# An attention and dense-layer kernel: interleaved q and k, four more pairs on DMA transposes and GpSimd pooling, attention ranked first

## Chip, cores, metric

The kernel runs on one core of one Trainium2 chip. The metric is device time in microseconds (us) of one execution. Before the change the median of three runs was 345.75 us (345.23 to 347.05).

## The reference, cut

Batch 8, 8 heads, 576 tokens, head size 64. Two attentions are added, and two dense layers follow.

```python
def _attn_ref(q, k, v):                       # each (8, 8, 576, 64)
    q_d = q.reshape(B, H, Sd, 4, D).mean(axis=3)      # pooled by 4: 144 tokens
    k_d, v_d = ...                                    # the same
    out_up = np.repeat(sm_attn(q_d, k_d, v_d), 4, axis=2)
    mask = np.abs(pos[:, None] - pos[None, :]) < 4    # a narrow band
    scores = np.where(mask, scale * q @ k.T, -1e9)
    ...                                               # softmax
    return out_up + attn @ v

def reference(**kwargs):
    x = attn_out.transpose(0, 2, 1, 3).reshape(4608, 512)
    h = x @ w_in                              # 512 x 2048
    return (h - np.tanh(h)) @ w_out           # 2048 x 512
```

## The kernel before

Two heads of one batch make a pair; there are 32 pairs. Each is loaded, reordered and cast (`qr`), transposed so that the head dimension lies on partitions, copied to `qk`, pooled by four in two additions (`half`, `qkd`), scored on TensorE, exponentiated on ScalarE (`E`), masked on VectorE (from pair 4 on; the first four add a bias on TensorE instead), multiplied with V, normalised (`ln`), transposed back and joined into `xT`, the input of the dense layers. From pair 16 on, DMA does the transposes, GpSimd pools V, and the join adds two SBUF operands. The parts that the argument touches:

```python
full = bass.AP(tensor=qk[s].tensor, ...,              # q, then k, 585 elements on
               ap=[qk[s].ap[0], [KOFF, 2], [1, 576]])
if p >= T_DMA:
    P.dma("SP", 1740, lambda: nc.sync.dma_start_transpose(out=qT[s], in_=qr[s]...), ...)
    for i in range(2):                                # one copy for q, one for k
        op("ACT", 600, lambda i=i: A.copy(out=full[:, i]..., in_=qT[s]...[:, i]), ...)
# ... else: nine TensorE transposes into PSUM and one copy from there
def add1(eng):                                        # first sum: half is (2, G, 2)
    eng.tensor_tensor(out=half, in0=four[:, :, :, 0:2], in1=four[:, :, :, 2:4], op=ALU.add)
def add2(eng):                                        # second sum: stores 288 elements in a row
    eng.tensor_tensor(out=qkd[s][:, 0:2 * G].rearrange("p (i g) -> p i g", i=2),
                      in0=half[:, :, :, 0], in1=half[:, :, :, 1], op=ALU.add)
# ...
if p >= NP:                                           # two mask multiplies a pair: 480+480, then 96+96
    op("DVE", 850, lambda: V.tensor_tensor(out=e1, in0=e1, in1=mask..., op=ALU.mult), ...)
# ... value matmuls, normalisation, transpose back
P.choice([("DVE", 850, lambda: join(V)), ("POOL", 1450, lambda: join(GP))], ...)
# ...
M2_FIRST, T_DMA, X_DMA, NEW = 16, 16, 16, 16
```

Nothing is scheduled at run time. `op` and `choice` record operations with a planned duration (the number) and a rank (`pri`); a list scheduler simulates the engines with those durations, picks the engine where there is a choice, and so fixes every engine's order.

The softmax here doesn't subtract the row's maximum and nothing guards it: scores larger than these inputs give would overflow.

## Time and profile before

| of the kernel before | value |
|---|---|
| median (range) of 3 runs | 345.75 us (345.23 to 347.05) |
| span of the profiled run | 345.9 us |
| value matmuls of pairs 4, 11, 15, 31 start at | 40.7, 92.7, 121.4, 240.4 us |
| dense matmuls in the order after the last value matmul | 468 of 1152 |
| second pooling sum on GpSimd | 711 ns, 29 of 32 |

The last value matmuls divide the run: until then attention and dense layers share TensorE; afterwards dense matmuls alone run at 0.216 us each. The span is the start of the last value matmuls, plus 0.216 us for each dense matmul left, plus some 5 us: here 240.4 + 101.1 + 4.4.

Two groups of the profile before that the prediction does not show, which matter later (columns: line, engine, operation, output<-inputs, shapes, count; busy us and mean ns of one; idle us just before and what ended it):

```profile
L497 POOL TENSOR_TENSOR qkd<-half 128x288 bf16<-128x288 f32 x29 | 20.6, 711 | 1.6 <-DVE half L492 0.7
...
L581 PE MATMUL ps_ox<-vw,E 128*128 128x65 bf16 x300 | 19.2, 194 | 4.6 <-DVE E L570 2.6 <-DVE E L556 1.9
```

The first is the second pooling sum. The second is TensorE's value matmuls, which sat idle 4.6 us in all for masks (L556, L570).

### The profile page before, as it was taken

To read this page: it belongs to the slowest core of one execution; us is meant where nothing else is said; L and a number is where in the kernel's file an instruction comes from. 1 tells how busy PE (TensorE), PEld (TensorE's weight loads), DVE (VectorE), ACT (ScalarE), POOL (GpSimd) and SP (SyncE) were. 2 spreads that over 40 slices of the span, in tenths; PEclk is the share of its full clock that TensorE was granted. 3 is DMA by queue.
4 is the path that set the end of the run, shared out by engine and by line. 5 is a ranking of instruction groups with operands and counts; after the bars stand their busy time and mean duration, and the time that the engine had idled before them with its cause. 6 is when DMAs were issued, how large, how long until landed. Compare 5 with 4: busy or idle time off the path is not lost.

```text
span 345.9 us, 6596 instructions
## 1 busy us (share of the span) xinstructions
PE 324.6 (94%) x2479; PEld 164.0 (47%) x2520; DVE 215.1 (62%) x341; ACT 217.4 (63%) x350; POOL 161.9 (47%) x191
## 2 busy tenths in 40 slices
PE   8888998899999999987989889999999999999995
PEld 4553555455555554443444444445444444444442
DVE  4786774258978577888789889876533443344300
ACT  2966864578888769978577878885443444344411
POOL 7675368364698729889666878641000000000000
PEclk9999999899999999999899999999999999999999
DMA  7999999999779926999999999532201100110021
GB/s 241 271 222 226 235 260 240 274 299 235 205 178 244 253 84 136 213 249 213 267 208 259 236 256 185 154 83 60 58 32 48 43 32 30 51 40 32 30 85 68
DMA packets 99213, 56.52 MB, mean 163 GB/s; under 512 B 77678, under 2 KB 86382, under 8 KB 99182
## 3 DMA queue, kind: packets, MB, share of 16 engines
q1 hardware_dynamic: 94670, 51.32, 60.2%
q0 software_dynamic: 4224, 4.19, 7.5%
q10 hardware_dynamic: 288, 0.59, 0.5%
q8 instruction: 19, 0.31, 0.4%
q14 instruction: 12, 0.10, 0.1%
HBM read 42.46 MB, written 9.44 MB: 150 GB/s over the span
## 4 chain that ended last, share of the span: by engine, by line
PE 66%; DVE 15%; DMA 9%; ACT 4%; issue 3%; POOL 2%; SPq 1%; POOLq 0%; ACTq 0%; DVEq 0%
PE ps_hy L690 27%; PE ps_hy L663 27%; DMA qkn<-in_k_dram 5%; DVE E L556 4%; DMA w_out_sb<-in_moe_w_out_dram 3%; DVE xT L626 2%; PE ps_ox L581 2%; DVE gT L674 2%; DVE ln L602 2%; PE ps_ts L511 2%; PE ps_ts L477 2%; PE ps_ox L588 2%; DVE xT L632 2%; ACT E L552 1%; DVE E L570 1%
## 5 line engine op out<-in xcount | busy, mean ns | idle before, releaser
L663 PE MATMUL ps_hy<-xT,w_in_sb 128*128 128x512 bf16 x555 | 142.4, 382 | 5.2 <-DVE xT L643 1.9
L690 PE MATMUL ps_hy<-w_out_sb,gT 128*128 128x512 bf16 x557 | 141.0, 382 | 3.4 <-DMA w_out_sb<-in_moe_w_out_dram 2.1
L674 DVE TENSOR_TENSOR gT<-ps_hy,u 128x512 bf16<-128x512 f32 x144 | 96.6, 685 | 72.4 <-ACT u L671 71.6
L671 ACT ACTIVATE u<-ps_hy 128x512 f32<-128x512 f32 x144 | 84.4, 600 | 70.8 <-PE ps_hy L663 69.7
L690 PEld LDWEIGHTS <-gT 128*128 128x128 bf16 x576 | 54.5, 98 | 64.5 <-issue 3.0
L663 PEld LDWEIGHTS <-w_in_sb 128*128 128x128 bf16 x576 | 53.6, 98 | 65.0 <-issue 6.3
L492 POOL TENSOR_TENSOR half<-qk 128x576 f32<-128x576 bf16 x29 | 33.7, 1161 | 28.8 <-ACT qk L468 13.7
L447 POOL CAST qr<-qkn 128x1152 bf16<-128x1152 f32 x28 | 33.5, 1198 | 14.7 <-PE ps_ts L477 9.6
L468 ACT COPY qk<-qT 128x576 bf16<-128x576 bf16 x32 | 38.1, 1213 | 0.0
L552 ACT ACTIVATE E<-ps_ts 128x960 bf16<-128x960 f32 x30 | 29.2, 973 | 11.6 <-PE ps_ts L511 11.3
L556 DVE TENSOR_TENSOR E<-E,mask 128x960 bf16<-128x960 bf16 x28 | 27.3, 974 | 13.3 <-ACT E L552 13.0
L602 DVE TENSOR_TENSOR ln<-ps_ox,r 128x896 bf16<-128x896 f32 x30 | 32.7, 1090 | 0.9
L701 ACT COPY y<-ps_hy 128x512 f32<-128x512 f32 x36 | 21.1, 586 | 18.3 <-PE ps_hy L690 14.1
L381 POOL CAST vw<-vst 128x640 bf16<-128x640 f32 x32 | 25.6, 799 | 8.7 <-DMA vst<-in_v_dram 7.1
L481 ACT COPY qk<-ps_ts 128x1152 bf16<-128x1152 bf16 x14 | 15.7, 1124 | 13.9 <-PE ps_ts L477 12.1
L581 PE MATMUL ps_ox<-vw,E 128*128 128x65 bf16 x300 | 19.2, 194 | 4.6 <-DVE E L570 2.6
L581 PEld LDWEIGHTS <-E 128*128 128x128 bf16 x320 | 16.1, 98 | 12.0 <-DVE E L556 4.0
L497 POOL TENSOR_TENSOR qkd<-half 128x288 bf16<-128x288 f32 x29 | 20.6, 711 | 1.6 <-DVE half L492 0.7
L402 POOL TENSOR_TENSOR v<-v 72x512 f32<-72x512 f32 x16 | 20.6, 1287 | 1.4 <-DMA v<-in_v_dram 0.5
L406 POOL TENSOR_TENSOR vp<-v 72x256 bf16<-72x256 f32 x16 | 12.3, 772 | 13.4 <-PE ps_ox L588 13.3
L511 PEld LDWEIGHTS <-qk 64*128 64x128 bf16 x320 | 9.6, 95 | 17.5 <-issue 16.7
L643 DVE TENSOR_TENSOR xT<-ps_ox,od 128x576 bf16<-128x576 bf16 x14 | 10.5, 752 | 8.0 <-ACT od L641 8.0
(90 smaller groups left out, 260.0 us busy)
## 6 DMA issues: line engine op xcount, KB each, us to landing
vst<-in_v_dram SPq DMA_DIRECT2D x62, 160.0 KB, 4.9
qkn<-in_q_dram SPq DMA_DIRECT2D x32, 288.0 KB, 4.7
out_dram<-y SPq DMA_DIRECT2D x36, 256.0 KB, 2.0
qkn<-in_k_dram SPq DMA_DIRECT2D x30, 288.0 KB, 4.6
v<-in_v_dram SPq DMA_DIRECT2D x16, 288.0 KB
w_in_sb<-in_moe_w_in_dram POOLq DMA_DIRECT2D x4, 512.0 KB, 11.1
w_out_sb<-in_moe_w_out_dram POOLq DMA_DIRECT2D x4, 512.0 KB, 10.4
qkn<-in_k_dram ACTq DMA_DIRECT2D x2, 288.0 KB, 3.4
```

Of the source, the lines that this page charges most:

```text
L381: P.choice([(eng, ns, lambda fn=fn: fn(out=vw[w][:, 2 * jj:2 * jj + 2, :, 0:64], in_=vst[s])) for eng, ns, fn in CAST_V[p >= NEARLY]], rea ...
L447: op("POOL", 1300, lambda: GP.tensor_copy(out=qr[s].rearrange("p a (h d) -> p h a d", h=2), in_=qkn[sn].rearrange("p h (a d) -> p h a d", ...
L468: op("ACT", 600, lambda i=i: A.copy(out=full[:, i].rearrange("p (g a) -> p g a", a=A9), in_=qT[s].rearrange("p a (g i) -> p i g a", i=2)[: ...
L492: eng.tensor_tensor(out=half, in0=four[:, :, :, 0:2], in1=four[:, :, :, 2:4], op=ALU.add)
L552: op("ACT", 870, lambda: A.activation(out=e1, in_=ps[:, :, 0:480], func=AF.Exp, scale=SCALE), reads=ts, writes=[("E", e, 0)], pri=pri)
L556: op("DVE", 850, lambda: V.tensor_tensor(out=e1, in0=e1, in1=mask[:, 0:480].unsqueeze(1).to_broadcast([128, 2, 480]), op=ALU.mult), reads= ...
L581: T.matmul(po[:, hh, 65 * t:65 * t + 65], E[e][:, c:c + 128], vw[w][:, 2 * jj + hh, t, :], start=True, stop=True)
L602: op("DVE", 1010, lambda: V.tensor_tensor(out=ln[s].rearrange("p n (h d) -> p h n d", d=D), in0=blocks[:, :, :, 0:64], in1=r[s].unsqueeze( ...
L663: T.matmul(ps_hy[slot], w_in_sb[:, dc, fc * 128:(fc + 1) * 128], xT[dc][:, kb * 512:kb * 512 + 512], start=(dc == 0), stop=(dc == N_DC - 1))
L671: op("ACT", 490, lambda: A.activation(out=u[us], in_=ps_hy[slot], func=AF.Tanh), reads=[("hy", slot)], writes=[("u", us)], pri=-1)
L674: op("DVE", 620, lambda: V.tensor_tensor(out=gT[g][:, fc, :], in0=ps_hy[slot], in1=u[us], op=ALU.subtract), reads=[("hy", slot), ("u", us) ...
L690: T.matmul(ps_hy[slot], gT[g][:, fc, ts * 128:ts * 128 + 128], w_out_sb[:, fc, :], start=(fc == 0), stop=(fc == N_FF - 1))
```

## The change

Four things at once. q and k are interleaved element by element, so that one copy fills both. Pairs 12 to 15 join the later ones in using DMA transposes, merged scores and GpSimd pooling of V. The dense layers' operations on ScalarE, VectorE and the DMA queue lose their rank before attention's (`DPRI`). And the planned durations are brought nearer to the trace. Core of the diff (line numbers shift by 2 or so; guards, keys and more planned durations are cut):

```diff
-    qk = fixed("qk", [128, 1192], BF16, 2)
+    qk = fixed("qk", [128, LEAD + 576 + 28, 2], BF16, 2)
-    half = fixed("half", [128, 2, G, 2], FP32)
+    half = fixed("half", [128, G, 2, 2], FP32)
...
-            for i in range(2):
-                op("ACT", 600, lambda i=i: A.copy(
-                    out=full[:, i].rearrange("p (g a) -> p g a", a=A9),
-                    in_=qT[s].rearrange("p a (g i) -> p i g a", i=2)[:, i]),
-                   reads=[("qT", s)], writes=[("qk", s, i)], pri=pri)
+            op("ACT", 1250, lambda: A.copy(
+                out=full.rearrange("p (g a) i -> p g a i", a=A9),
+                in_=qT[s].rearrange("p a (g i) -> p g a i", i=2)),
+               reads=[("qT", s)], writes=[("qk", s)], pri=pri)
...
-            eng.tensor_tensor(out=half, in0=four[:, :, :, 0:2],
-                              in1=four[:, :, :, 2:4], op=ALU.add)
+            eng.tensor_tensor(out=half, in0=four[:, :, 0:2, :],
+                              in1=four[:, :, 2:4, :], op=ALU.add)
...
-                eng.tensor_tensor(out=qkd[s][:, 0:2 * G].rearrange("p (i g) -> p i g", i=2),
-                                  in0=half[:, :, :, 0],
-                                  in1=half[:, :, :, 1], op=ALU.add)
+                eng.tensor_tensor(out=qkd[s][:, 0:2 * G].rearrange("p (i g) -> p g i", i=2),
+                                  in0=half[:, :, 0, :],
+                                  in1=half[:, :, 1, :], op=ALU.add)
...
-            T.matmul(sc[:, c:c + NQ[t]], qk[s][rows, k0:k0 + 128],
-                     qk[s][rows, QW * t:QW * t + NQ[t]], ...)
+            T.matmul(sc[:, c:c + NQ[t]], qk[s][rows, k0:k0 + 128, 1],
+                     qk[s][rows, q0:q0 + NQ[t], 0], ...)
...
-            P.choice([("DVE", 850, lambda: join(V)), ("POOL", 1450, lambda: join(GP))],
+            P.choice([("DVE", 1900, lambda: join(V)), ("POOL", 1400, lambda: join(GP))],
...
-           reads=[("hy", slot)], writes=[("u", us)], pri=-1)
+           reads=[("hy", slot)], writes=[("u", us)], pri=DPRI)
...
-    M2_FIRST, T_DMA, X_DMA, NEW = 16, 16, 16, 16
+    M2_FIRST, T_DMA, X_DMA, NEW, LATE = 12, 12, 12, 12, 0
+    DPRI = 5000
```

The second sum: its input now has q and k side by side, its output still has all of q before all of k. With `p g i` as the order, it stores q of group 0, then k of group 0, then q of group 1, and so on.

More of the change, by code (lines that the diff above doesn't have):

```diff
@@ L208 @@
     NQ = [120, 120, 120, 120, 96]
-    KOFF = 585
+    LEAD = 4
     N_FF = Dff // 128
@@ L442, in attention @@
         cold = 1.5 if p < NP else 1.0
+        late = LATE if p >= 2 * NP else 0
         yield
@@ L458, in attention @@
                      pri=pri - 12)
-        full = bass.AP(tensor=qk[s].tensor, offset=qk[s].offset,
-                       ap=[qk[s].ap[0], [KOFF, 2], [1, 576]])
+        full = qk[s][:, LEAD:LEAD + 576]
         if p >= T_DMA:
@@ L478, in attention @@
             P.fresh.add(len(P.ops))
-            op("PE", 520 * cold, tr, reads=[("qr", s, 0), ("qr", s, 1), "ident"],
+            op("PE", 520 * cold, tr, slack=late, reads=[("qr", s, 0), ("qr", s, 1), "ident"],
                writes=ts, pri=pri)
             op("ACT", 1240, lambda: A.copy(
-                out=full.rearrange("p i (g a) -> p i g a", a=A9),
-                in_=b16.rearrange("p (a g i) -> p i g a", a=A9, i=2)),
-               reads=ts,
-               writes=[("qk", s, 0), ("qk", s, 1)], pri=pri)
-        four = full.rearrange("p i (g a) -> p i g a", a=4)
+                out=full.rearrange("p (g a) i -> p g a i", a=A9),
+                in_=b16.rearrange("p (a g i) -> p g a i", a=A9, i=2)),
+               reads=ts, writes=[("qk", s)], pri=pri)
+        four = full.rearrange("p (g a) i -> p g a i", a=4)
         adders = ADDERS[p >= NEARLY]
         def add1(eng):
-            eng.tensor_tensor(out=half, in0=four[:, :, :, 0:2],
-                              in1=four[:, :, :, 2:4], op=ALU.add)
+            eng.tensor_tensor(out=half, in0=four[:, :, 0:2, :],
+                              in1=four[:, :, 2:4, :], op=ALU.add)
         def add2(eng):
             with nc.allow_low_precision("pooled q and k"):
-                eng.tensor_tensor(out=qkd[s][:, 0:2 * G].rearrange("p (i g) -> p i g", i=2),
-                                  in0=half[:, :, :, 0],
-                                  in1=half[:, :, :, 1], op=ALU.add)
+                eng.tensor_tensor(out=qkd[s][:, 0:2 * G].rearrange("p (i g) -> p g i", i=2),
+                                  in0=half[:, :, 0, :],
+                                  in1=half[:, :, 1, :], op=ALU.add)
         P.choice([(name, n1, lambda eng=eng: add1(eng)) for name, n1, _, eng in adders],
-                 reads=[("qk", s, 0), ("qk", s, 1)], writes=["half"], pri=pri)
+                 reads=[("qk", s)], writes=["half"], pri=pri)
         P.choice([(name, n2, lambda eng=eng: add2(eng)) for name, _, n2, eng in adders],
@@ L509, in score @@
             rows = slice(64 * hh, 64 * hh + 64)
-            k0 = KOFF + QW * t - 4
-            T.matmul(sc[:, c:c + NQ[t]], qk[s][rows, k0:k0 + 128],
-                     qk[s][rows, QW * t:QW * t + NQ[t]], start=p >= NP, stop=p >= NP or t >= 3)
+            k0, q0 = LEAD + QW * t - 4, LEAD + QW * t
+            T.matmul(sc[:, c:c + NQ[t]], qk[s][rows, k0:k0 + 128, 1],
+                     qk[s][rows, q0:q0 + NQ[t], 0], start=p >= NP, stop=p >= NP or t >= 3)
         def biased(lo, hi):
@@ L539, in s12 @@
             s2(po.rearrange("p n c -> p (n c)"), 72)
-        qks = [("qk", s, i) for i in range(2)]
+        qks = [("qk", s)]
         yield
@@ L544, in attention @@
         if new:
-            op("PE", 620, s12, reads=qks + [("qkd", s)], writes=ts + ox, pri=pri)
+            op("PE", 620, s12, slack=late, reads=qks + [("qkd", s)], writes=ts + ox, pri=pri)
         else:
-            op("PE", 420 * cold + 600 * (p < NP), s1,
+            op("PE", 420 * cold + 600 * (p < NP), s1, slack=late,
                reads=qks + ["bias"] * (p < NP), writes=ts, pri=pri)
@@ L551, in attention @@
         e3 = E[e][:, 1152:1728].rearrange("p (h c) -> p h c", h=2)
-        op("ACT", 870, lambda: A.activation(
+        op("ACT", 960, lambda: A.activation(
             out=e1, in_=ps[:, :, 0:480], func=AF.Exp, scale=SCALE),
@@ L555, in attention @@
         if p >= NP:
-            op("DVE", 850, lambda: V.tensor_tensor(
+            op("DVE", 950, lambda: V.tensor_tensor(
                 out=e1, in0=e1,
@@ L561, in attention @@
         if not new:
-            op("PE", 380 * cold + 150 * (p < NP), s2, reads=qks + [("qkd", s)], writes=ts, pri=pri)
-        op("ACT", 240, lambda: A.activation(
+            op("PE", 380 * cold + 150 * (p < NP), s2, slack=late, reads=qks + [("qkd", s)], writes=ts, pri=pri)
+        op("ACT", 310, lambda: A.activation(
             out=e2v, in_=ps2[:, :, 0:96], func=AF.Exp, scale=SCALE),
            reads=ts2, writes=[("E", e, 1)], pri=pri)
-        op("ACT", 560, lambda: A.activation(
+        op("ACT", 650, lambda: A.activation(
             out=e3, in_=ps2[:, :, 96:384], func=AF.Exp, scale=SCALE / 16.0),
@@ L569, in attention @@
         if p >= NP:
-            op("DVE", 300, lambda: V.tensor_tensor(
+            op("DVE", 450, lambda: V.tensor_tensor(
                 out=e2v, in0=e2v,
@@ L594, in attention @@
         P.fresh.add(len(P.ops))
-        op("PE", 570 * cold, outs,
+        op("PE", 570 * cold, outs, slack=late,
            reads=[("E", e, 0), ("E", e, 1), ("E", e, 2), ("vw", w, jj),
@@ L601, in attention @@
            reads=ox, writes=[("r", s)], pri=pri)
-        op("DVE", 1010, lambda: V.tensor_tensor(
+        op("DVE", 1060, lambda: V.tensor_tensor(
             out=ln[s].rearrange("p n (h d) -> p h n d", d=D),
@@ L636, in join @@
                     op=ALU.add)
-            P.choice([("DVE", 850, lambda: join(V)), ("POOL", 1450, lambda: join(GP))],
+            P.choice([("DVE", 1900, lambda: join(V)), ("POOL", 1400, lambda: join(GP))],
                      reads=[("lT", s)], writes=[("x", b, j)], pri=pri)
             return
-        op("PE", 370 * cold, back, reads=[("ln", s)], writes=ox, pri=pri)
+        op("PE", 370 * cold, back, slack=late, reads=[("ln", s)], writes=ox, pri=pri)
         op("ACT", 190, lambda: A.copy(out=od[s], in_=px[1][:, 0:144]),
@@ L670, in mm1 @@
                writes=[("hy", slot)], pri=5000)
-        op("ACT", 490, lambda: A.activation(
+        op("ACT", 590, lambda: A.activation(
             out=u[us], in_=ps_hy[slot], func=AF.Tanh),
-           reads=[("hy", slot)], writes=[("u", us)], pri=-1)
-        op("DVE", 620, lambda: V.tensor_tensor(
+           reads=[("hy", slot)], writes=[("u", us)], pri=DPRI)
+        op("DVE", 670, lambda: V.tensor_tensor(
             out=gT[g][:, fc, :], in0=ps_hy[slot], in1=u[us], op=ALU.subtract),
-           reads=[("hy", slot), ("u", us)], writes=[("gT", g, fc)], pri=-1)
+           reads=[("hy", slot), ("u", us)], writes=[("gT", g, fc)], pri=DPRI)
     ycur = {}
@@ L700, in mm2 @@
             yn[0] += 1
-            op("ACT", 490, lambda: A.copy(out=y[ys], in_=ps_hy[slot]),
-               reads=[("hy", slot)], writes=[("y", ys)], pri=-1)
+            op("ACT", 590, lambda: A.copy(out=y[ys], in_=ps_hy[slot]),
+               reads=[("hy", slot)], writes=[("y", ys)], pri=DPRI)
             r0 = kb * 512 + ts * 128
             P.dma("SP", 530, lambda: nc.sync.dma_start(
-                out=out[r0:r0 + 128, :], in_=y[ys]), 700, 344, src=[("y", ys)], pri=-1)
+                out=out[r0:r0 + 128, :], in_=y[ys]), 700, 344, src=[("y", ys)], pri=DPRI)
     def dense(kb):
@@ L745, in guards @@
         def guards(i=i):
-            V.memset(qk[i][:, 576:585], 0.0)
-            V.memset(qk[i][:, 1161:1192], 0.0)
+            V.memset(qk[i][:, 0:LEAD], 0.0)
+            V.memset(qk[i][:, LEAD + 576:LEAD + 604], 0.0)
         op("DVE", 200, guards, pri=-98,
-           writes=[("qk", i, a) for a in range(2)])
+           writes=[("qk", i)])
     for i in range(NVW):
```

## The prediction

> **What bounds the kernel now.** I read the page's busy shares and slices first, then a table of stretches, then the groups by line, then the chain of waits.
>
> From the page: busy shares, then the span in 40 slices of 8.65 us.
>
> ```profile
> PE 324.6 (94%) x2479; PEld 164.0 (47%) x2520; DVE 215.1 (62%) x341; ACT 217.4 (63%) x350; POOL 161.9 (47%) x191
> ...
> PE   8888998899999999987989889999999999999995
> ...
> POOL 7675368364698729889666878641000000000000
> PEclk9999999899999999999899999999999999999999
> DMA  7999999999779926999999999532201100110021
> ```
>
> TensorE is busy all along, at full clock but for two slices; GpSimd works until slice 28 (240 us); the DMA engines are full until about slice 25, with a dip at 14 and 15 (121 to 138 us). So there are two phases: attention with the dense layers mixed in, then dense layers alone. The table of stretches, cut where the value matmuls (L581) of pairs 11, 15 and 31 start in the timeline (92.7, 121.4, 240.4 us), gives busy time and number of instructions of each engine, then clock, DMA share and GB/s:
>
> ```profile
> 27.50:92.70 65.20, 62.10 (x566) 34.14 (x576) 41.27 (x66) 44.94 (x77) 35.26 (x40) 0.97 1.04 251
> 92.70:121.40 28.70, 28.38 (x266) 15.51 (x268) 20.80 (x33) 23.56 (x39) 24.62 (x26) 1.00 0.91 220
> 121.40:240.40 119.00, 111.15 (x917) 54.78 (x932) 97.10 (x139) 93.13 (x142) 81.48 (x86) 0.99 0.86 189
> 240.40:342.10 101.70, 101.17 (x477) 46.26 (x485) 36.53 (x56) 38.52 (x67) 0.56 (x2) 1.00 0.12 44
> ```
>
> The last row is the bare rate: the built program's order has 468 dense matmuls of 512 columns after the last value matmul, 101.1 us at 0.216 us each (chain of waits: x8 in 1.73 us). The kernel is **TensorE work plus TensorE's holes**: all 1152 dense matmuls are 248.8 us, attention's own TensorE work some 60 (16 pairs x 2.74 + 16 x 1.05, both worked out below), and the rest of 346 us is holes, start and a 3.8 us tail. The third row shows where a hole can be saved: pairs 16 to 31 take 119 us, in which the order has 412 dense matmuls (89.0 us) and 16 x 1.05 us of attention (16.8; in the timeline merged scores take 0.48, values 0.57), so 13.2 us, 0.83 us per pair, are holes. The second row, pairs 12 to 15 with TensorE transposes, has hardly any.
>
> Groups by line (count | busy us, mean ns of one | idle before it and its releaser):
>
> ```profile
> L468 ACT COPY qk<-qT 128x576 bf16<-128x576 bf16 x32 | 38.1, 1213 | 0.0
> L481 ACT COPY qk<-ps_ts 128x1152 bf16<-128x1152 bf16 x14 | 15.7, 1124 | 13.9 <-PE ps_ts L477 12.1 <-POOL qr L447 1.8
> L402 POOL TENSOR_TENSOR v<-v 72x512 f32<-72x512 f32 x16 | 20.6, 1287 | 1.4 <-DMA v<-in_v_dram 0.5
> L556 DVE TENSOR_TENSOR E<-E,mask 128x960 bf16<-128x960 bf16 x28 | 27.3, 974 | 13.3 <-ACT E L552 13.0
> L626 DVE TENSOR_TENSOR xT<-lT 128x480 bf16<-128x480 bf16 x11 | 12.8, 1167 | 1.6 <-DMA lT<-ln 1.6
> L626 POOL TENSOR_TENSOR xT<-lT 128x480 bf16<-128x480 bf16 x5 | 5.1, 1012 | 7.8 <-DMA lT<-ln 7.8
> ```
>
> The first two rows are the oddity that the interleaving is after: two copies of 576 elements from SBUF cost 2.43 us, one of 1152 from PSUM 1.12. The chain in this phase runs mostly through VectorE:
>
> ```profile
> 161.93 2.13 DVE E L556
> ...
> 177.05 2.62 DVE xT L626
> ```
>
> The same mask multiply takes 0.64 us at its shortest and 2.76 at its longest, the join 0.65 to 2.62 (view of one line). So in pairs 16 to 31 VectorE (97.1 of 119 us), slowed by something, makes TensorE's holes.
>
> [...] 216 start to start in the dense runs, 56 inside the nine transposes. [...] In L468 each two-byte element read lies 256 bytes from the next; 2.1 ns per element against 0.98 for L481[...]. [...]
>
> **The change, part by part.**
> 1. *TensorE transposes removed for pairs 12 to 15.* In the timeline near 84 to 93 us: nine transposes into PSUM 0.51 us (92.24 to 92.75), seven back 0.75 (89.56 to 90.31), V pooling 0.66 per two pairs, so 0.33, and split scores 0.58 against merged 0.48. Together 1.69 us a pair, 6.8 us in all. It lies on TensorE, the bound.
> 2. *What these pairs take on.* GpSimd: V pooling, 1.29 + 0.77 us a pair. VectorE or GpSimd: a join (VectorE 1.17 + 0.74, GpSimd 1.01 + 0.35) for the PSUM join (0.75). DMA: 0.82 MB more a pair, by the tiles' sizes: V again 0.295, transpose in 0.295, out 0.229. They also take on the holes of the later pairs: 4 x 0.5 to 0.8 us, 2 to 3 us. Net of parts 1 and 2: some 4 us gained.
> 3. *Interleaving.* One ScalarE copy (I take 1.2 us) for two (2.43): 16 x 1.2 = 19 us of ScalarE, beside other work. On the path it shortens the wait GpSimd's half sums have for it (11.1 us in five waits between 140 and 240 us), so the scores come earlier. GpSimd's sums keep their sizes; the second now writes strided, and I leave it at 0.71.
> 4. *Order.* Joins in the order: VectorE 11 to 10, GpSimd 5 to 10, of 20 now. Attention before dense on every engine, and planned times raised to what the trace has (mask 850 to 950 ns against 974 measured; tanh 490 to 590 against 600), so the static order should stall TensorE less. Dense matmuls before the last value matmul: 684 to 720; after it 468 to 432.
>
> The sum, at value matmuls: pair 4 starts at 40.7 us and pair 11 at 92.7 before; the order has 184 dense matmuls by then, and 188 after: I keep 92.5. Pairs 12 to 15: 110 dense x 0.216 = 23.8, attention 4.2, holes 4 x 0.6 = 2.4: 30.4. Pairs 16 to 31: 422 x 0.216 = 91.2, attention 16.8, holes 16 x 0.5 = 8: 116. The end: 432 x 0.216 = 93.3, plus 4.4 for the last values and the last copy and store as before. Total 336.6, say **337 us**, 2.5% less. The choice in it is 0.5 us of holes a pair, for 0.83.
>
> **The rivals.**
> *The DMA engines become the bound.* From 140 to 220 us they moved 18.5 MB at 232 GB/s with a share of 1.07: full. Between pair 12's start and the last one's end the new program must move about 14.7 MB of q, k, v, 5.9 of V again, 10.5 of transposes and 4.3 of output: 35.4 MB, 153 us at 232 GB/s, against the 146 us planned. For it: the full slices. Against: waits on loads are short (V window 1.3 us in that phase), four pairs are loaded ahead, and DMA has room in slices 14 and 15 (2 and 6 tenths), where the added transfers fall. It would give about 343.
> *GpSimd becomes the bound.* Per pair 1.20 + 1.16 + 0.71 + 0.80 + 1.29 + 0.77 = 5.93, plus half a join 0.68: 6.6 of the planned 7.3 us, and a fuller GpSimd blocks VectorE more. If it keeps 1 us of waits a pair, 20 pairs take 152 us for 146: again about 343. Against: its waits were mostly for the ScalarE copy that is halved.
> *The holes nearly close*, as the priorities intend: 0.2 us a pair saves 6 us more, 331.
> *Strided operands slow the matmuls*: twice the 0.48 us of scores would add up to 14 us. Little speaks for it.
>
> **Range and chances.** 330 to 344 holds the closed holes at one end and either full engine at the other. Faster by over 2% means below 338.8; my centre is 1.8 us under that and the two rivals that end at 343 are each real: 0.57 faster, 0.38 within, 0.05 slower.
>
> **What would show it.** L468 as 20 copies of 1152 near 1.2 us. Score matmuls at unchanged spacing. Last value matmul at 237 to 241 us, with 93 us of pure dense after. Holes below 0.6 us a pair from 120 us on. The prediction is wrong if GpSimd is over 95% busy between 93 and 239 us, if waits on loads or on the transposes grow above some 10 us, or if mask multiplies average above 1.1 us.

## The result, and the profile after

The changed kernel took **356.19 us** (median of 3 runs, 355.33 to 358.14): slower by 3%. Ratios are the mean time of one kernel's fast runs over that of the other's of the same rounds, so not quite the ratio of the medians quoted; here 1.0305, with a 95% interval of 1.0224 to 1.0385. Executions over 1.5% slower than the fastest of the same kernel are left out of the means. The two profiles may be compared.

From the page of the changed kernel: busy us and share of each engine, then tenths of 40 slices of 8.9 us.

```profile
PE 319.9 (90%) x2404; PEld 161.2 (45%) x2444; DVE 236.9 (66%) x334; ACT 198.2 (56%) x328; POOL 196.7 (55%) x210
...
PE   7774999999998968789988979699999999999995
...
POOL 6765545859969888986977688889200000000000
PEclk9996899999999999999999999899999999999999
DMA  7999998699999999999999998733320100010021
```

TensorE's and ScalarE's work went down, as intended, but VectorE gained 22 us and GpSimd 35 (236.9 for 215.1, 196.7 for 161.9). GpSimd now works until slice 28 of longer slices, 258 us. Holes show in TensorE's row from slice 12 to 25, where before it was mostly 9s and 8s. The deepest hole is earlier, in slice 3 (4 tenths, at a granted clock of 6 tenths).

The same four stretches as in the prediction, cut where the value matmuls of pairs 11, 15 and 31 start in this kernel (97.1, 131.5, 258.1 us): busy us and number of instructions of PE, PEld, DVE, ACT and POOL, then clock, DMA share and GB/s.

```profile
20.00:97.10 77.10, 69.43 (x642) 39.26 (x652) 52.31 (x74) 50.33 (x86) 53.20 (x54) 0.93 1.05 229
97.10:131.50 34.40, 29.10 (x242) 14.58 (x244) 29.96 (x35) 22.57 (x36) 29.30 (x28) 1.00 1.11 232
131.50:258.10 126.60, 112.17 (x919) 55.96 (x936) 108.17 (x136) 78.22 (x128) 100.60 (x100) 0.99 0.91 195
258.10:352.00 93.90, 93.42 (x442) 42.71 (x449) 33.62 (x51) 35.04 (x61) 0.10 (x1) 1.00 0.13 45
```

In the second row TensorE idles 5.3 of 34.4 us, in the third 14.4 of 126.6. VectorE is busy 87 and 85% of these two, GpSimd 85 and 79%, neither all of the time. The account of the loss: attention ends at 258.1 us in place of 240.4 (17.7 later); 432 dense matmuls are left in place of 468 (36 x 0.216 = 7.8 us less); 17.7 - 7.8 = 9.9. The spans (356.4 and 345.9) differ by 10.5, since what comes on top of the dense matmuls at the end is 5.0 us for 4.4.

Groups by line, the answers to those of before (L495 to L497, L554 to L556, L467 to L468, L568 to L570, L579 to L581, L624 to L626):

```profile
L495 POOL TENSOR_TENSOR qkd<-half 128x288 bf16<-128x288 f32 x30 | 46.5, 1551 | 1.4 <-DVE half L490 0.7
L554 DVE TENSOR_TENSOR E<-E,mask 128x960 bf16<-128x960 bf16 x28 | 39.0, 1392 | 12.1 <-ACT E L550 12.1
...
L467 ACT COPY qk<-qT 128x1152 bf16<-128x1152 bf16 x20 | 24.3, 1214 | 0.0
L568 DVE TENSOR_TENSOR E<-E,mask 128x192 bf16<-128x192 bf16 x28 | 20.7, 740 | 2.5 <-ACT E L561 2.5
L579 PE MATMUL ps_ox<-vw,E 128*128 128x65 bf16 x300 | 20.2, 197 | 16.7 <-DVE E L554 9.8 <-DVE E L568 5.6 <-ACT qk L467 1.3
L624 DVE TENSOR_TENSOR xT<-lT 128x480 bf16<-128x480 bf16 x10 | 18.7, 1867 | 0.5 <-DMA lT<-ln 0.5
```

Three things stand out. The second sum takes 1551 ns where it took 711: 25 us more of GpSimd (30 x 0.84). The mask multiply takes 1392 ns for 974, and the join on VectorE 1867 for 1167, although their operands have not changed. And the value matmuls idled 16.7 us for 4.6, 15.4 of them for masks. The one copy costs 1214 ns for 1152 elements, as much as each of the two did for 576: that part worked.

In the chain of waits (start us, us, what), the pieces that are masks and joins have grown to match, up to 5.35 us for a multiply that can take 0.64 (the second line is of dense matmuls):

```profile
29.28 3.46 DVE E L554
33.47 3.57 PE ps_hy L661 x8
...
192.51 2.83 DVE E L554
...
199.84 2.77 DVE xT L624
...
224.13 5.35 DVE E L554
```

The first two of these lines show a loss of its own kind, before pair 4. The mask multiply at 29.28 takes 3.46 us, the join of an early pair stands behind it on VectorE, and the dense matmuls at 33.47 wait 4.24 us for that join, TensorE's longest single wait. From 27 to 36 us the granted clock averages 0.69, for 1.00 before. At pair 4's value matmuls the changed kernel is 8.1 us behind (48.8 us for 40.7), at pair 11's 4.4 (97.1 for 92.7). With the same order and the sums packed (e1 below) pair 4 starts at 42.0 us. The profiled run is the slowest of the three (358.14 us).

### The profile page after: what moved, and what is told of

It is laid out like the page before. It is cut to its first block, busy times and chain, and to the rows that moved or that the text cites.

```text
span 356.4 us, 6457 instructions
## 1 busy us (share of the span) xinstructions
PE 319.9 (90%) x2404; PEld 161.2 (45%) x2444; DVE 236.9 (66%) x334; ACT 198.2 (56%) x328; POOL 196.7 (55%) x210
## 4 chain that ended last, share of the span: by engine, by line
PE 66%; DVE 22%; ACT 4%; issue 2%; DMA 2%; POOL 2%; SPq 1%; POOLq 0%; ACTq 0%
PE ps_hy L688 28%; PE ps_hy L661 27%; DVE E L554 7%; DVE xT L624 4%; DVE E L568 3%; DVE gT L672 3%; PE ps_ox L579 3%; ACT E L550 2%; PE ps_ts L509 2%; DVE xT L630 2%; DMA qkn<-in_k_dram 2%; PE ps_ox L586 2%; DVE ln L600 2%; PE ps_ts L476 1%; PE ps_ox L420 1%
## 5 line engine op out<-in xcount | busy, mean ns | idle before, releaser
L495 POOL TENSOR_TENSOR qkd<-half 128x288 bf16<-128x288 f32 x30 | 46.5, 1551 | 1.4 <-DVE half L490 0.7
L554 DVE TENSOR_TENSOR E<-E,mask 128x960 bf16<-128x960 bf16 x28 | 39.0, 1392 | 12.1 <-ACT E L550 12.1
L448 POOL CAST qr<-qkn 128x1152 bf16<-128x1152 f32 x28 | 35.3, 1260 | 2.3 <-PE ps_ts L476 2.3
L550 ACT ACTIVATE E<-ps_ts 128x960 bf16<-128x960 f32 x30 | 29.1, 970 | 11.3 <-PE ps_ts L509 11.2
L579 PE MATMUL ps_ox<-vw,E 128*128 128x65 bf16 x300 | 20.2, 197 | 16.7 <-DVE E L554 9.8
L699 ACT COPY y<-ps_hy 128x512 f32<-128x512 f32 x36 | 21.3, 591 | 24.1 <-PE ps_hy L688 24.0
L381 POOL CAST vw<-vst 128x640 bf16<-128x640 f32 x32 | 28.4, 886 | 0.7 <-DMA vst<-in_v_dram 0.7
L579 PEld LDWEIGHTS <-E 128*128 128x128 bf16 x320 | 16.7, 100 | 25.9 <-DVE E L554 14.8
L406 POOL TENSOR_TENSOR vp<-v 72x256 bf16<-72x256 f32 x20 | 15.2, 758 | 20.3 <-PE ps_ox L586 15.7
L402 POOL TENSOR_TENSOR v<-v 72x512 f32<-72x512 f32 x20 | 25.5, 1274 | 1.2
L467 ACT COPY qk<-qT 128x1152 bf16<-128x1152 bf16 x20 | 24.3, 1214 | 0.0
L568 DVE TENSOR_TENSOR E<-E,mask 128x192 bf16<-128x192 bf16 x28 | 20.7, 740 | 2.5 <-ACT E L561 2.5
L624 DVE TENSOR_TENSOR xT<-lT 128x480 bf16<-128x480 bf16 x10 | 18.7, 1867 | 0.5 <-DMA lT<-ln 0.5
L480 ACT COPY qk<-ps_ts 128x1152 bf16<-128x1152 bf16 x10 | 11.2, 1118 | 10.2 <-PE ps_ts L476 10.2
```

Of the source, the lines that this page charges most:

```text
L448: op("POOL", 1300, lambda: GP.tensor_copy(out=qr[s].rearrange("p a (h d) -> p h a d", h=2), in_=qkn[sn].rearrange("p h (a d) -> p h a d", ...
L550: op("ACT", 960, lambda: A.activation(out=e1, in_=ps[:, :, 0:480], func=AF.Exp, scale=SCALE), reads=ts, writes=[("E", e, 0)], pri=pri)
L554: op("DVE", 950, lambda: V.tensor_tensor(out=e1, in0=e1, in1=mask[:, 0:480].unsqueeze(1).to_broadcast([128, 2, 480]), op=ALU.mult), reads= ...
L579: T.matmul(po[:, hh, 65 * t:65 * t + 65], E[e][:, c:c + 128], vw[w][:, 2 * jj + hh, t, :], start=True, stop=True)
L624: eng.tensor_tensor(out=x0.rearrange("p (t g a) -> p t g a", t=4, a=4), in0=lT[s][:, 0:4, 0:QW].rearrange("p t (g a) -> p t g a", a=4), in ...
```

## The experiments

After this result the theory was **S**: the second sum, slowed by its store, cost the time. How it reaches TensorE became theory **V**: VectorE's masks and joins are held up longer behind GpSimd (1392 ns for 974, 1867 for 1167), and the value matmuls wait for masks. The rivals: **B**, GpSimd itself paces the pairs; the other parts of the change are to blame (pairs 12 to 15, ranks, DMA: **D**); and the static order came out badly (**O**, **P**, **M** in the expectations). Later came **Q**, that joins ahead of masks in VectorE's queue explain the order's part, and **R**, that the second sum's changed reads are the cost and not its store.

Runs of kernels sent together share their runs of the kernel before (medians 345.1 to 347.6 us), so ratios to it compare better than times. One of its runs took 663 us; it counts as slow and is in no ratio. For the main versions the profile's three marks are:

| version | ratio to before (95%) | median us | masks and joins over their shortest, us | last values start, us | dense left |
|---|---|---|---|---|---|
| before | 1 | 345.75 | 28.3 | 240.4 | 468 |
| changed kernel | 1.0305 (1.0224 to 1.0385) | 356.2 | 53.5 | 258.1 | 432 |
| e1, sums packed | 0.9981 (0.9910 to 1.0051) | 347.2 | 40.8 | 248.4 | 432 |
| e16, pooled interleaved | 1.0017 (0.9960 to 1.0074) | 345.6 | 39.2 | 248.0 | 432 |
| e4, all but interleaving | 0.9819 (0.9753 to 0.9885) | 341.5 | 30.3 | 242.4 | 428 |
| e11, e4's order, jumping store | 1.0099 (1.0027 to 1.0171) | 347.9 | 45.3 | 248.5 | 428 |
| e10, e4's order, packed | 0.9799 (0.9734 to 0.9864) | 338.6 | 35.8 | 241.0 | 428 |
| e17, e4's order, pooled interleaved | 0.9861 (0.9807 to 0.9914) | 340.3 | 29.3 | 239.3 | 428 |

The fourth column sums, over all mask multiplies and VectorE joins of the trace, what each took above the shortest of its shape (0.65 us for the large ones, 0.245 for the small).

### Which part costs: e1 to e4

**e1: only the two sums packed.** Everything else, and every engine's order, is the changed kernel's.

```diff
-    half = fixed("half", [128, G, 2, 2], FP32)
+    half = fixed("half", [128, 2, G, 2], FP32)
-        four = full.rearrange("p (g a) i -> p g a i", a=4)
+        four = full.rearrange("p (g a) i -> p i g a", a=4)
...
-                eng.tensor_tensor(out=qkd[s][:, 0:2 * G].rearrange("p (i g) -> p g i", i=2),
-                                  in0=half[:, :, 0, :], in1=half[:, :, 1, :], op=ALU.add)
+                eng.tensor_tensor(out=qkd[s][:, 0:2 * G].rearrange("p (i g) -> p i g", i=2),
+                                  in0=half[:, :, :, 0], in1=half[:, :, :, 1], op=ALU.add)
```

> The changed kernel with one edit: the pooled q and k are summed with the q/k index outermost, so the second sum (GpSimd, 30 of 32) stores contiguously again as in the kernel before; every engine's order of instructions is the same as in the changed kernel. Theory S (the strided store of the second sum, 1551 ns against 711 before, x30 = 25 us of GpSimd, is what cost the time): the second sum falls to 0.66 to 0.72 us, mask multiplies fall from 1392 to about 1000 ns mean, and the time falls to 335 to 343 us. Rival O (the new order, attention before dense, or the planned costs, make the holes): the second sum falls but the time stays above 350. Rival D (earlier DMA transposes fill the DMA engines): 345 to 352, with waits on loads or transposes left.

Measured: 347.2 us (345.8 to 348.4). Its group of the second sum:

```profile
L495 POOL TENSOR_TENSOR qkd<-half 128x288 bf16<-128x288 f32 x30 | 20.9, 698 | 1.4 <-DVE half L490 0.7
```

The access patterns of the two sums, none of them on TensorE, are worth 9 us by the medians, 3% of the whole. The loss against before is gone, but the gain predicted is not there either: S had expected 335 to 343 us and masks near 1000 ns, and they average 1207. The store is then not the whole loss. The time lies in D's range, but the waits for transposes (7.5 us at joins on GpSimd, 6.4 in the changed kernel) did not fall with it, and e10 below is faster with the same transfers.

**e2: before, with the interleaving alone** (jumping store included), and **e3: e2 with the sums packed.** The edits are the layout hunks of the diff above, and e1's.

> The kernel before with the interleaved q and k alone (strided store of the second sum included; DMA transposes from pair 16, old ranks, old planned costs). Theory S: the second sum takes about 1.5 us here too and the time is 350 to 358 us, so the loss comes with this part alone. Rivals O and D: within 2 us of the kernel before, 343 to 348.

> The kernel before with interleaved q and k, and the second sum stored contiguously. Theory S: 341 to 346 us; the single ScalarE copy of 1.2 us for two of 1.21 saves 19 us of ScalarE beside the path, so little or nothing of the time. If strided operands slowed the score matmuls, over 347 and a wider spacing of the score matmuls.

Measured: e2 363.2 us (360.1 to 366.6), ratio 1.0413 (1.0321 to 1.0505); e3 345.1 us (344.1 to 350.4), ratio 0.9909 (0.9830 to 0.9988). e2 is slower than S expected. "Alone" holds for the edit, not for the order: planned with one copy for two, e2 and e3 get an order that is not that of the kernel before (10 joins on VectorE for 11), but the same for both. So the store is cleanly priced between the two, at 5%; the 0.9% that e3 gains on before is layout and order together.

**e4: the changed kernel with the old layout of q and k** (the layout hunks undone).

> The changed kernel with the old layout of q and k (two copies of 576, contiguous sums): DMA transposes, merged scores and V pooled on GpSimd from pair 12, attention before dense, new planned costs. Theory S: 337 to 343 us, as the prediction had it for these parts. Rivals O and D: 350 or more, since their cause is all here.

Measured: 341.5 us (340.7 to 342.4), ratio 0.9819. So the scheduling parts together gain 1.8%, where 2.5% was predicted for the whole. The loss comes with the interleaving and the order that its plan brings, and in e1 part of it remains although the store is mended. That remainder is taken up under the order below.

### The store or the reads: e16, e17

e1 changed what the second sum reads as well as how it stores. e16 changes the store alone: the pooled q and k stay interleaved too, so 288 elements are stored in a row, and the pooled scores read every second element. To stay inside the new tile, pooled keys are read 104 at a time instead of 128 from pair 12 on (72 are used).

```diff
-    qkd = fixed("qkd", [128, 344], BF16, 2)
+    qkd = fixed("qkd", [128, 176, 2], BF16, 2)
-                eng.tensor_tensor(out=qkd[s][:, 0:2 * G].rearrange("p (i g) -> p g i", i=2),
+                eng.tensor_tensor(out=qkd[s][:, 0:G],
...
-                    T.matmul(sc[:, c:c + G], qkd[s][rows, k0:k0 + 128],
-                             qkd[s][rows, 0:G], start=True, stop=True)
+                    T.matmul(sc[0:n, c:c + G], qkd[s][rows, k0:k0 + n, 1],
+                             qkd[s][rows, 0:G, 0], start=True, stop=True)
```

> The changed kernel with the pooled q and k kept interleaved as well (two values side by side, the pooled scores read every second element), so that the second sum reads exactly what it reads in the changed kernel and stores 288 elements in a row instead of jumping 288 bytes between them; every engine's order stays the changed kernel's, and the weight loads of the pooled scores are 104 columns wide instead of 128. Theory S, the jumping store is the cost: second sum near 0.70 us, time as with packed sums, 345 to 349. Rival R, its reads of the first sum's pairs are the cost: second sum stays near 1.55 us and the time near 356.

> The same in the order of the schedule-only kernel, in which the packed sums took 338.6 and the jumping store 347.9 us. Theory S: second sum near 0.70 us and 337 to 341 us. Rival R: near 1.55 and 348.

Measured: e16 345.6 us (343.3 to 348.1), e17 340.3 us (338.5 to 343.6), both within what S expected. The second sum in e16:

```profile
L495 POOL TENSOR_TENSOR qkd<-half 128x288 bf16<-128x288 f32 x30 | 21.4, 712 | 0.7
```

Same reads as in the changed kernel, 712 ns for 1551: the jump of the store is the cost. R falls. VectorE agrees: its few second sums took 1831 to 1996 ns with the jump (1882 in the changed kernel, where there are two; also e6, e11, e12) and 620 to 1055 with a store in a row (622 in e1, 818 in e16; also before, e4, e9, e10, e17). Each can include a wait for GpSimd.

### The way from GpSimd to TensorE: e1's timeline, e12, e5

How the longer sum reaches TensorE can be read even in e1, where it is short. A timeline (start us, us, engine, line, operation; in brackets idle before it):

```profile
198.87 5.75 DVE L624 TENSOR_TENSOR xT<-lT 128x480 bf16<-128x480 bf16 x1
...
199.06 1.14 POOL L490 TENSOR_TENSOR half<-qk 128x576 f32<-128x576 bf16 x1
...
200.15 1.14 POOL L448 CAST qr<-qkn 128x1152 bf16<-128x1152 f32 x1
...
201.26 0.66 POOL L495 TENSOR_TENSOR qkd<-half 128x288 bf16<-128x288 f32 x1
...
201.87 1.14 POOL L448 CAST qr<-qkn 128x1152 bf16<-128x1152 f32 x1
...
202.97 1.14 POOL L490 TENSOR_TENSOR half<-qk 128x576 f32<-128x576 bf16 x1
...
204.72 0.65 DVE L554 TENSOR_TENSOR E<-E,mask 128x960 bf16<-128x960 bf16 x1
...
205.42 0.37 PE L579 MATMUL ps_ox<-vw,E 128*128 128x65 bf16 x5 [1.40 <-DVE E L554]
```

A join that can take 0.65 us starts at 198.87 and ends at 204.62. GpSimd works without a gap until 204.11; the join ends 0.51 us later. It did not slip in when one GpSimd instruction ended and the next began. The mask behind it, though itself quick (0.65 us), starts at 204.72, and TensorE's value matmuls start at 205.42 after 1.40 us of idling. The join lasted through six GpSimd instructions in a row, the one that was running when it started (until 199.10, not shown) and five more (GpSimd's records overlap here by 0.03 to 0.05 us, so their ends are rough by as much).

The whole traces bear this out. All that masks and joins took over their shortest (53.5 us in the changed kernel, 40.8 in e1, 28.3 before) lies inside running GpSimd instructions. Sorted by the instruction that was running, the second sum has 19.3 us of it in the changed kernel for 7.0 in e1, and 11.3 in e11 (below) for 4.2 in e10: nearly all of the difference between the changed kernel and e1, and most of that between e11 and e10. VectorE did not always wait for the end of the jumping sum, though: counted back from their ends, eight of the changed kernel's masks and joins got to work 0.82 to 1.46 us after one had started, while it ran on.

**e12: the changed kernel without the two mask multiplies** (wrong result, relative error 0.93; the plan still counts them, so all orders stay).

```diff
-            op("DVE", 950, lambda: V.tensor_tensor(out=e1, in0=e1, in1=mask..., op=ALU.mult), reads=...
+            op("DVE", 950, None, reads=["mask"], writes=[("E", e, 0)], pri=pri)
```

(and the same for the second mask.)

> The changed kernel, strided store and order kept, without VectorE's mask multiplies (a wrong result on purpose: the local scores are not masked from pair 4 on). Theory V (the store costs time through VectorE: mask multiplies that read two SBUF tensors are held up by a fuller GpSimd, and TensorE's value matmuls wait for them): 332 to 342 us with the strided store still at 1.5 us. Rival B (GpSimd itself is full and paces attention): 348 to 356, with GpSimd over 95% busy from 93 us to the end of attention.

Measured: 343.9 us (343.0 to 344.7), ratio 0.9969 (0.9894 to 1.0043): between the ranges of V and B.

```profile
L495 POOL TENSOR_TENSOR qkd<-half 128x288 bf16<-128x288 f32 x30 | 45.1, 1505 | 2.9 <-DVE half L490 2.3
...
L573 PE MATMUL ps_ox<-vw,E 128*128 128x65 bf16 x300 | 18.3, 194 | 0.8 <-ACT E L561 0.8
```

The second sum is nearly as slow as ever, GpSimd does the same work (83% busy from 121.7 to 243.6 us, where B expected over 95%), and yet attention ends at 243.6 us in place of 258.1, with the value matmuls' idling down from 16.7 to 0.8 us. So GpSimd's own pace does not force 258: B falls, and the way through VectorE's masks is shown. The run also takes the masks' own 25 us of VectorE away (28 x 0.895), so its 12 us are not all blocking.

**e5: e1 with the V casts of pairs from 4 on moved from GpSimd to ScalarE**, to relieve GpSimd another way.

```diff
-              [("POOL", 820, GP.tensor_copy)]]
+              [("ACT", 750, A.copy)]]
```

> e1_packed_sums with the cast of V (0.8 us a pair, 28 pairs) moved from GpSimd to ScalarE, which the changed kernel leaves 44% idle. If GpSimd's load is what starves VectorE and holds TensorE: the time lost by masks and joins falls from 41 to under 25 us and the kernel falls to 333 to 341 us. If the DMA engines or TensorE itself bind, it stays at 345 to 348.

Measured: 351.0 us (348.8 to 353.3), ratio 1.0156 (1.0070 to 1.0242): slower than e1, and than either side expected. Masks and joins lost 28.9 us for e1's 40.8, and attention ended at 232.3 us for 248.4, as V has it; but the plan, with another engine loaded, had put only some 644 dense matmuls before that point and left about 508. 76 more at 0.216 us give back 16 us, all that was won. The work of an engine and the plan cannot be changed apart here, which leads to the last question.

### The static order: e10, e11, e9, e6, e7, e8

e1 and e4 do nearly the same work, yet e4 is 5.7 us faster by its median. The orders differ, though, and for a small cause: the plan has two copies of 600 ns in e4, one of 1250 in e1. **e10 is e1's work planned as e4**: two planned copies of 600, the second of which emits nothing. Every engine's order is then e4's. **e11 puts the jumping store back into e10.**

```diff
-            op("ACT", 1250, lambda: A.copy(
-                out=full.rearrange("p (g a) i -> p g a i", a=A9),
-                in_=qT[s].rearrange("p a (g i) -> p g a i", i=2)),
-               reads=[("qT", s)], writes=[("qk", s)], pri=pri)
+            for i in range(2):
+                op("ACT", 600, None if i else lambda: A.copy(
+                    out=full.rearrange("p (g a) i -> p g a i", a=A9),
+                    in_=qT[s].rearrange("p a (g i) -> p g a i", i=2)),
+                   reads=[("qT", s)], writes=[("qk", s, i)], pri=pri)
```

> Interleaved q and k with contiguous sums as in e1_packed_sums, but planned with the two copies of e4_schedule_only, so that every engine's order is exactly that of e4; the one copy of 1.2 us stands where the first of the two stood. It asks where the 5.7 us between e1 (347.2) and e4 (341.5) come from. Theory P (the order: where the joins and masks fall against GpSimd's runs of instructions): 338 to 343 us. Theory G (the shorter copy lets GpSimd run without gaps, and VectorE's two-input instructions[...] starve): 345 to 349, with the time lost by masks and joins near e1's 41 us instead of e4's 30.

> e10_order_of_e4 (338.6 us) with the strided store of the second sum put back, order unchanged. If the store's own time costs what it cost between e1 and the changed kernel (347.2 to 356.2), this is 345 to 350 us. If the order decides and the store does not, 337 to 341.

Measured: e10 338.6 us (337.3 to 340.2), the fastest version and faster than both kernels; e11 347.9 us (347.3 to 350.2). The four stretches of e10, cut at the same value matmuls (91.0, 120.2, 241.0 us):

```profile
20.00:91.00 71.00, 66.79 (x630) 36.53 (x630) 47.10 (x73) 48.57 (x83) 45.20 (x51) 0.98 1.14 251
91.00:120.20 29.20, 28.32 (x240) 14.12 (x238) 23.96 (x34) 20.38 (x35) 24.15 (x26) 1.00 1.11 238
120.20:241.00 120.80, 114.57 (x946) 56.62 (x946) 101.60 (x142) 79.95 (x130) 93.13 (x99) 1.00 0.98 213
241.00:334.00 93.00, 93.00 (x447) 42.33 (x445) 32.87 (x51) 34.95 (x61) 0.19 (x1) 1.00 0.13 46
```

This is near the picture that the prediction drew: 29.2 us for pairs 12 to 15 (30.4 predicted), 120.8 for the rest (116), 97.5 from there to the end of the span (97.7). The DMA share of 1.11 and 0.98 did no harm. Six versions now form a table of store against order (median us):

| second sum | changed kernel's order | e4's order |
|---|---|---|
| stored 288 bytes apart | 356.2 (the change) | 347.9 (e11) |
| in a row, by packing | 347.2 (e1) | 338.6 (e10) |
| in a row, interleaved | 345.6 (e16) | 340.3 (e17) |

Down a column the store costs 7.7 to 10.6 us, across a row the order 5.4 to 8.6; by the ratios to before, 2.4 to 3.2% and 1.6 to 2.1%. They add up.

**e9: e10 with its one copy done twice**, to price the saved copy.

```diff
-                op("ACT", 600, None if i else lambda: A.copy(
+                op("ACT", 600, lambda: A.copy(
```

> The same order and layout, but the ScalarE copy of 1.2 us is done twice (the second is waste), so q and k arrive as late as in e4. Theory G: within 2 us of e4, 340 to 343, so faster than e10 although it does more. Theory P: the same as e10 or up to 2 us slower.

```profile
L468 ACT COPY qk<-qT 128x1152 bf16<-128x1152 bf16 x40 | 48.5, 1212 | 2.8 <-DMA qT<-qr 2.2
L491 POOL TENSOR_TENSOR half<-qk 128x576 f32<-128x576 bf16 x29 | 33.3, 1148 | 43.5 <-ACT qk L468 21.4 <-ACT qk L481 16.7 <-DMA qkn<-in_q_dram 4.1
```

Measured: 343.3 us (341.9 to 344.3), ratio 0.9930 (0.9866 to 0.9994) for 0.9799, 4.7 us slower than e10, which neither theory expected. GpSimd's first sums wait 21.4 us for this copy in place of 5.6 in e10. So one copy less on the path is worth 1.3%, and that part of the change's intent is sound. e4, with two copies of 576, is at 0.9819, within the interval of e10: against that pair of copies a gain from the interleaving is not separated.

**e6: the changed kernel with the second sum's planned time set to what it takes** (the slow store kept).

```diff
-    ADDERS = [[("DVE", 700, 420, V), ("POOL", 1150, 750, GP)],
-              [("POOL", 1150, 750, GP)]]
+    ADDERS = [[("DVE", 700, 1900, V), ("POOL", 1150, 1550, GP)],
+              [("POOL", 1150, 1550, GP)]]
```

> The changed kernel, strided store kept, with the plan told its true cost (1550 ns for the second sum on GpSimd, 1900 on VectorE). Theory S says that GpSimd's time itself is the cost: 352 to 357 us, at most 4 us better than the changed kernel. Rival M (the order, planned for a 0.75 us sum, is what goes wrong): 340 to 348.

Measured: 346.9 us (344.4 to 348.0), ratio 1.0031 (0.9941 to 1.0120), with the second sum at 1572 ns: what rival M expected, not S. A truer plan gives back 9 us although the work is the same. It is another order, so this is no proof that the truth of the plan did it.

**e7: before with only pairs 12 to 15 moved; e8: e4 with that undone**, so only the ranks and planned durations are left.

```diff
-    M2_FIRST, T_DMA, X_DMA, NEW = 16, 16, 16, 16
+    M2_FIRST, T_DMA, X_DMA, NEW = 12, 12, 12, 12
```

> The kernel before with only the four pairs moved: DMA transposes, merged scores and V pooling on GpSimd from pair 12 on; old layout, ranks and planned costs. The prediction's parts 1 and 2 say 4 us less: 340 to 344 us. If the DMA engines bind, 346 to 350.

> The kernel before with only the ranks and the planned costs of the change (attention before dense, measured durations in the plan); transposes from pair 16, old layout. If the order alone closes holes: 340 to 344 us. If it does not: 345 to 349.

Measured: e7 363.5 us (361.4 to 365.7), ratio 1.0540; e8 355.1 us (353.0 to 356.1), ratio 1.0288: both above everything expected of them. Each part alone loses, together (e4) they gain 1.8%. e7's plan left 526 dense matmuls after the last values, e8's 492, in place of 428; e7 also has a stretch with a hole and a lower clock:

```profile
182.00:212.00 30.00, 22.08 (x204) 11.33 (x205) 24.20 (x31) 19.39 (x28) 24.15 (x25) 0.88 1.15 237
212.00:242.00 30.00, 24.14 (x198) 12.23 (x203) 24.25 (x37) 22.20 (x35) 18.74 (x20) 0.78 0.58 146
```

TensorE is busy 22.1 of 30 us in the first row; in its order, two pairs follow each other there with no dense work between. In the second it is busy 24.1 of 30 us and the granted clock averages 0.78. The guess is an order with too little dense work at hand, but no run isolates that, nor what the lower clock comes from.

### What in the order: e13, e14, e15

In the changed kernel's order, 8 of VectorE's 10 joins stand just ahead of mask multiplies, so a held-up join holds up the mask, as in the timeline above (the mask starts 0.10 us after the join's end). Theory Q says that this is what its order costs. e13 is e1, e14 is e10, e15 is the changed kernel, each with only those joins put behind the masks on VectorE:

```diff
+    def behind(self, order):      # for each VectorE join: move it past the masks that follow at once
+        ...
+            if last is not None:
+                order.insert(last, order.pop(at))
+        return order
...
-        order = self.order()
+        order = self.behind(self.order())
```

> e1_packed_sums (347.2 us) with nothing changed but VectorE's order: a join that stands just ahead of mask multiplies is put behind them (8 of its 10 joins). Theory Q (joins ahead of masks are what this order loses by): 339 to 343 us, and TensorE's waits of the value matmuls for masks fall to less than half. If not: 345 to 349, and the 8.5 us stay open.

> e10_order_of_e4 (338.6 us) with the same swap, which moves 5 of its 12 joins. Theory Q: 1 to 4 us less, 334.5 to 338. If not: 338 to 341.

> The changed kernel itself, strided store kept, with the same swap. Theory Q: 347 to 351 us, that is the store's 9 us left and the order's 8.5 mostly gone. If not: 354 to 358.

Measured: e13 343.4 us (342.8 to 346.4), ratio 0.9939 for e1's 0.9981; e14 341.0 us (338.4 to 342.1), 0.9825 for e10's 0.9799; e15 355.9 us (354.5 to 358.2), 1.0288 for the changed kernel's 1.0305. In e14, 5 of 12 joins moved. Only e13's median moves the right way by more than a microsecond, by 3.8 us, and its interval overlaps e1's. In e13 the joins lost 2.4 us for e1's 14.5, but the masks 29.5 for 26.2: the delay moved to the masks, and value matmuls waited 8.1 us for them of 11.0, where Q asked for less than half. Q falls as the general cause. What exactly costs the changed kernel's order 5.4 to 8.6 us against e4's **stays open**; the time is lost in attention (248.4 against 241.0 us at its end in e1 and e10), at value matmuls that wait for masks: they idled 11.0 us in e1 and 3.2 in e10.

## Why the prediction was wrong, point by point

- **One copy of about 1.2 us for two: right.** 1214 ns, 20 of them. That it lies partly on the path was right too (e9).
- **Interleaved operands do not slow the score matmuls: right.** All score matmuls on `qk` (320) take 12.2 us before and 12.4 after, summed from each start to the next; their median is 213 and 212 ns.
- **468 to 432 dense matmuls after the last values: right**, and worth its 7.8 us.
- **"GpSimd's sums keep their sizes; the second now writes strided, and I leave it at 0.71": this step failed.** It was 1551 ns. The same reads with a store in a row took 712 (e16). The text had seen the stride and took it as free for want of a number, though it had itself set L468's 2.1 ns an element, for 0.98 in L481, beside reads of two-byte elements 256 bytes apart. It cost 7.7 to 10.6 us of time.
- **"so the static order should stall TensorE less", and from it "0.5 us of holes a pair, for 0.83": failed for this order.** By the prediction's own sum the holes became 1.2 us a pair from pair 16 on (126.6 - 91.2 - 16.8 = 18.6 us) and 1.6 in pairs 12 to 15 (34.4 - 23.8 - 4.2 = 6.4). The order that two planned copies give is faster by 5.4 to 8.6 us, and with it and the store mended the kernel took 338.6 us, 1.6 above the prediction (e10). That the total came so near is partly luck: e10's last 16 pairs took 120.8 us for 116 (0.67 us of holes a pair), and what came before was 2.7 us shorter than predicted. The "holes" are not all idle time either: before, the sum makes 13.2 us of them where the prediction's own table has TensorE idle for 7.9, and for pairs 12 to 15 it gives 30.0 us (88 dense matmuls, 4 x 2.74) where they took 28.7. That the ranks and times make a better order was an assumption: alone they lose 2.9% (e8).
- **Where the 19.2 us went** between the predicted end of attention (92.5 + 30.4 + 116 = 238.9) and the measured 258.1: 4.6 us before pair 11, where the slow sum also runs and the start loses (above); 4.0 in pairs 12 to 15 (34.4 for 30.4); 10.6 in pairs 16 to 31 (126.6 for 116).
- **The rival "GpSimd becomes the bound" was half right.** Its clause that "a fuller GpSimd blocks VectorE more", for which the prediction had no run, fits the two traces: with GpSimd busy 196.7 us for 161.9, masks and joins took 53.5 us over their shortest for 28.3, all of it inside running GpSimd instructions. Its account of 6.6 us of 7.3 a pair becomes 7.4 with the true second sum, which would have made it the main line. But GpSimd was near 85 and 79% busy in the two stretches, not over 95, and without masks it kept up (e12).
- **The mark set in advance worked**: "if mask multiplies average above 1.1 us" was given as a sign of failure; they averaged 1.39.
- **The DMA rival fell**: the share was 1.11 in the second stretch, but the waits for the transposes out came to 6.4 us at joins on GpSimd, and e10, with the same transfers and the same share, took 338.6 us.

## What to carry to other kernels

When a layout changes, follow it through to every instruction that reads or writes it, and price each new access pattern, also on engines that are not the bound: here a store that jumps from element to element doubled one GpSimd instruction (711 to 1551 ns), and VectorE's mask multiplies (1392 ns for 974) carried the delay to TensorE, whose value matmuls idled 15.4 us for them, for 4.5. Where a plan fixes the order, judge an edit of the work with the order held (record the planned operations as before, and let one emit nothing), since here planning one copy of 1250 ns or two of 600 moved the result by 5.4 to 8.6 us, where the whole change was meant to save 8.8. A gain that is predicted from a better order should be counted as a chance, not as a sum.
